# Order and places of the V-half moves in a fused attention and token-mixing kernel

## The chip, the cores and the metric

The kernel runs on one core of one Trainium2 chip. A core has a matrix engine (TensorE, "PE" in the profile; its weight loads are shown apart as "PEld"), a vector engine (VectorE, "DVE"), a scalar engine for activations (ScalarE, "ACT"), a general engine (GpSimd, "POOL"), and a sync engine (SyncE, "SP") that in this kernel does nothing but issue DMA transfers. Each engine works through its own instruction queue in order and waits on semaphores for the others.

The metric is the device time of one execution in microseconds, taken as the median over several runs.

## The reference

The input x has 2048 tokens of width 512, in bfloat16. Two branches are computed from it and mixed by a gate for each token:

```python
g = sigmoid((x * gate_w).sum(-1, keepdims=True))
a = attention(x)      # 32 heads of width 16, sliding window of 256 tokens, causal
b = token_mlp(x)      # layernorm, then a two-layer MLP over the token axis, hidden size 1376, gelu
return g * a + (1 - g) * b
```

The attention projects x to q, k and v with one 512 x 1536 matrix. A query at token i sees the keys at i-255 to i. Its softmax output is multiplied by wo (512 x 512). The token MLP multiplies by w1 (2048 x 1376) and w2 (1376 x 2048) along the token axis.

## The kernel before

**Tiles.** Tokens are cut into 16 tiles of 128. The attention's queries are handled in blocks j that are shifted by half a tile, so that block j has the queries of the tokens 128 j + 64 to 128 j + 191. Such a block needs the keys of tile j whole ("A") and of tile j-1 whole ("B"), with a triangle masked away in part of each, and two corners ("C"): the first 64 keys of tile j+1 ("D"), and the last 64 keys of tile j-2 ("F"). For each block the score products `s` run on PE, the exponentials `e` on ACT, the masks `m` on DVE or POOL, then the products with V, named `pvj.0` to `pvj.3` (line 1158, with the matmuls at line 1087), and then the steps `n1` to `n4` on DVE, which transpose, normalise and put the output into the tile `xo`. `n1` (line 1178) is what reads the PV products' accumulator.

**V's halves.** V lies in the tile `VA`, one slot for each token tile, 17 columns for each head (16 of V and a column of ones, which gives the softmax's denominator). For a block with both corners (j = 2 to 14), the two corners are multiplied together: the weights for one head are a column of 128 rows whose upper 64 rows come from the first half of V's tile j+1 and whose lower 64 rows come from the second half of tile j-2. There are two forms of it, each with the other half of the rows blank, and they lie in a tile `VZ` with three places (`NVZ = 3`, line 354). The blanks are written once (lines 580 and 581). For each block one task `vzj` (lines 725 to 732) issues two DMA transfers from `VA` to `VZ`, of 64 partitions each:

```python
nc.sync.dma_start(buf(b)[0:HB, 0, :], VA[0:HB, t_, :]),            # line 727, t_ = j + 1
nc.sync.dma_start(buf(b)[HB:P, 1, :], VA[HB:P, t_ - 3, :]),        # line 728, tile j - 2
```

The task waits for the copies `vc` that bring V's tiles j+1 and j-2 from PSUM into `VA` (line 709), for the blanks, and for its place: a place is free again when the PV products of the block that had it before are done. The readers of a place are the steps `pvj.1` and `pvj.3`, those of the "B" halves (lines 1149 to 1156); their matmuls and weight loads are the ones on `VZ` at line 1087.

**Order.** The order of the work on each engine is written out by hand, as five strings of task names in `PLAN` (lines 189 to 277). A digit after a colon is the place of a ring that the task takes: `vz6:0` is the move for block 6, into place 0 of `VZ`. The function `arrange` (line 85) walks the five queues with a table of estimated costs. It never changes the order within a queue; it only merges the five queues into one order of emission, in which dependences are then worked out. The estimated times have one more use (lines 1325 to 1330): where a POOL task's start is estimated within 1 us of the end of a DVE task that uses both of DVE's ports, a wait of POOL on that task is added.

**The SP queue.** It starts with loads of x, the weights and w1 (names `w1_gi`: column group g, token quarter i), between which the half swaps `vs` and the first `vz` moves stand. Then come the loads of w2 (`w2_0` to `w2_2`), which go into the space of w1 and so wait until the first MLP layer's products `u` on that group are done, the load of wo, and the stores of the outputs (`o0` to `o15r`), each of which waits for its last step `f` on DVE or ACT. Between these the remaining `vz` moves stand. As every queue, SP's is in order: a `vz` task whose place isn't free yet holds up all that stands behind it.

Before the change the 13 moves take the places like this: place 2 belongs to `vz12` alone, which is issued third; place 1 to `vz2`, `vz3`, `vz8` and `vz14`; place 0 to the other eight (4, 5, 6, 7, 9, 10, 11, 13).

On PE the second half of the schedule mixes the attention of later blocks with the MLP's second layer (`y` chains, line 669, also the line of the projections and of the first layer). The PV products run in the order of the blocks.

Of the kernel before, what the change touches and what calls it, by code (L numbers as in the profile page):

```python
# [84 lines left out]
def arrange(tasks):  # L85
# [21 lines left out]
    while len(order) < len(tasks):  # L107
# [163 lines left out]
    """,  # L271
    SP="""
        x0.0 x0.2 wqk0 wqk1 wqk2 wqk3 x1.4 xt1 wv x2.8 bias xt3 x3.12 xt2 vs0 w1_02 w1_03 vs1 w1_22 vs2 gw w1_12
        w1_23 w1_01 w1_00 w1_10 w1_11 vz2:1 w1_13 vz12:2 vz4:0 vz3:1 w1_20 w1_21 vz8:1 vz5:0 vz6:0 w2_0 vz7:0 w2_1
        w2_2 vz9:0 wo o0 o4 vz14:1 o8 o7 vz10:0 vs13 o2 o9 o1 vz11:0 o5 o10 vz13:0 o11 o3 o6 o12 o14 o13 o15l o15r
    """,
)

# [1096 lines left out]
```

## Time and profile before

| what | value |
|---|---|
| time, median of 4 runs | 200.53 us (199.89 to 201.4) |
| the profiled execution | 199.89 us, span 198.2 us from the first instruction to the last |
| granted TensorE clock | 1.000 |
| busy in the span: PE, ACT, DVE, POOL | 188.7, 169.4, 156.5, 79.8 us |
| moves to `VZ` | 26 DMA issues of 70.0 KB, 2.5 us in the median from issue to landing |
| loads of weights from `VZ` on PE | 832, 13.2 us busy |

The table's busy times are those of the page's first part. An engine's idle time is listed with the instruction before which it lay and with what released it; the queue of SP is listed by itself ("SPq"), as starts and durations of the DMA issues, and its waits are not part of any engine's idle time. A time "to landing" runs from the start of the issue to the transfer's end. In the timeline, starts are in us from the start of the span; a matmul's line is "output <- moving operand, weights".

### The profile page before, as it was taken

What the parts mean: (1) busy time and instruction counts of PE and PEld (TensorE: products, weight loads), DVE (VectorE), ACT (ScalarE), POOL (GpSimd) and SP (SyncE); (2) the same over time, 40 slices, a digit from 0 to 9 for tenths busy, and PEclk for the clock granted to TensorE, in tenths of its full rate; (3) what the DMA queues carried; (4) which work ended last, traced back from release to release, by engine and by line L of the source; (5) the groups of instructions that cost most, each with busy time, mean ns of one, the idle gap of its engine ahead of it and who ended that gap; (6) DMA issues with size and microseconds to landing.
All of it is one profiled execution on the core that took longest, in us unless ns stands there. A gap on an engine that the chain in (4) does not pass through costs nothing. (4 is left out here: it accounts for less than half of the span.)

```text
span 198.2 us, 9066 instructions
## 1 busy us (share of the span) xinstructions
PE 188.7 (95%) x4026; PEld 93.2 (47%) x4058; DVE 156.5 (79%) x318; ACT 169.4 (85%) x198; POOL 79.8 (40%) x118
## 2 busy tenths in 40 slices
PE   7999999999999999999999999999999999999993
PEld 3644444443535445445534554344445354554572
DVE  1898988879988978985689789636767868869683
ACT  2379999999897997998899899899899989899632
POOL 6395897326325351113323200055069335551310
PEclk9999999999999999999999999999999999999999
DMA  5999899940061001001499760010212020100002
GB/s 166 297 291 217 180 279 332 329 135 5 3 174 32 3 0 32 3 5 32 126 345 385 275 185 7 26 55 30 67 38 71 18 71 19 33 30 29 31 7 79
DMA packets 23189, 22.02 MB, mean 111 GB/s; under 512 B 7566, under 2 KB 21262, under 8 KB 23150
## 3 DMA queue, kind: packets, MB, share of 16 engines
q1 hardware_dynamic: 23150, 21.44, 37.0%
q8 instruction: 32, 0.52, 1.1%
q14 instruction: 7, 0.06, 0.1%
HBM read 15.61 MB, written 2.10 MB: 89 GB/s over the span
## 5 line engine op out<-in xcount | busy, mean ns | idle before, releaser
L893 ACT ACTIVATE et<-ps 128x1024 bf16<-128x1024 f32 (+1 forms) x94 | 89.6, 1017 | 6.0 <-PE ps L941 2.2
L535 POOL TENSOR_SCALAR_AFFINE_SELECT et<-et 128x512 bf16<-128x512 bf16 (+2 forms) x63 | 46.6, 750 | 55.4 <-ACT et L893 34.6
L893 ACT ACTIVATE XT<-ps 128x1024 bf16<-128x1024 f32 (+1 forms) x60 | 58.3, 1013 | 7.8 <-PE ps L941 4.7
L669 PEld LDWEIGHTS <-wb 128*32 128x32 bf16 (+4 forms) x645 | 31.9, 97 | 34.5 <-issue 6.5
L669 PE MATMUL pb<-ug,wb 128*32 128x512 bf16 (+5 forms) x377 | 43.8, 366 | 1.1 <-issue 1.0
L669 PE MATMUL pb<-h,wb 128*128 128x512 bf16 (+2 forms) x251 | 42.6, 381 | 1.3 <-issue 1.3
L535 POOL TENSOR_SCALAR_AFFINE_SELECT XT<-XT 128x512 bf16<-128x512 bf16 (+1 forms) x28 | 20.0, 719 | 47.1 <-ACT XT L893 28.1
L669 PE MATMUL pb<-XT,wqkv 128*128 128x512 bf16 (+2 forms) x184 | 31.1, 370 | 1.3 <-ACT XT L893 0.4
L1178 DVE STREAM_TRANSPOSE et<-ps 128x1024 f32<-128x1024 f32 (+1 forms) x17 | 20.1, 1183 | 12.3 <-PE ps L1087 11.6
L1087 PEld LDWEIGHTS <-VA 128*32 128x32 bf16 (+1 forms) x1056 | 20.1, 97 | 6.5 <-issue 1.3
L941 PE MATMUL ps<-QZ,KT 32*128 32x256 bf16 (+1 forms) x496 | 23.1, 265 | 0.0
L753 DVE TENSOR_TENSOR QZ<-pb,par 128x1024 bf16<-128x1024 f32 x16 | 19.5, 1221 | 2.4 <-PE pb L669 2.3
L669 PEld LDWEIGHTS <-wqkv 128*128 128x128 bf16 (+1 forms) x190 | 12.6, 97 | 14.5 <-DMA wqkv<-in_A_wqkv_dram 0.5
L1087 PE MATMUL ps<-et,VA 128*32 128x128 bf16 (+2 forms) x624 | 18.0, 218 | 0.0
L669 PE MATMUL pb<-wo,xo 128*32 128x512 bf16 (+2 forms) x148 | 17.2, 375 | 0.2
L941 PEld LDWEIGHTS <-KT 32*128 32x128 bf16 x496 | 7.4, 92 | 20.6 <-ACT et L893 10.6
L669 PE MATMUL pb<-wqkv,XT 128*128 128x512 bf16 (+1 forms) x65 | 15.4, 380 | 0.8 <-issue 0.5
L973 DVE TENSOR_TENSOR et<-et,mask 128x512 bf16<-128x512 bf16 x26 | 13.3, 510 | 2.5 <-ACT et L893 2.4
L440 DVE TENSOR_SCALAR ot<-pb,c,c 128x512 bf16<-128x512 f32 (+1 forms) x11 | 8.6, 784 | 7.4 <-PE pb L669 7.4
L1087 PE MATMUL ps<-XT,VA 128*32 128x128 bf16 (+2 forms) x432 | 13.9, 215 | 0.0
L1087 PEld LDWEIGHTS <-VZ 128*32 128x32 bf16 x832 | 13.2, 98 | 0.9 <-DMA VZ<-VA 0.3
L769 DVE BATCH_NORM_STATS2 stats<-xo 128x6 f32<-128x512 bf16 x16 | 10.8, 683 | 3.3 <-DMA xo<-in_A_x_dram 3.3
(76 smaller groups left out, 199.4 us busy)
## 6 DMA issues: line engine op xcount, KB each, us to landing
wb<-in_B_w_dram SPq DMA_DIRECT2D x8, 512.0 KB, 8.3
wb<-in_B_w_dram SPq DMA_DIRECT2D x2, 2048.0 KB
VZ<-VA SPq DMA_DIRECT2D x26, 70.0 KB, 2.5
xo<-in_A_x_dram SPq DMA_DIRECT2D x3, 512.0 KB, 5.4
out_dram<-ot SPq DMA_DIRECT2D x12, 128.0 KB, 2.1
wb<-in_B_w_dram SPq DMA_DIRECT2D x4, 352.0 KB, 5.8
wqkv<-in_A_wqkv_dram SPq DMA_DIRECT2D x4, 256.0 KB, 4.6
wb<-in_B_w_dram SPq DMA_DIRECT2D x1, 1024.0 KB, 5.4
```

The source lines that it names most:

```text
L440: return nc.vector.tensor_scalar(out=out_, in0=in_, scalar1=scale, scalar2=bias, op0=ALU.mult, op1=ALU.add)
L535: return nc.gpsimd.affine_select(out=out_, in_=in_, pattern=[[0, n] for n in pattern] + [[step, HB]], compare_op=op, fill=0.0, base=base_, ...
L669: made.append(nc.tensor.matmul(buf(b)[c:z_, c0:c0 + w_], lhsT=lhsT[:, c:z_], rhs=rhs, start=(j == 0), stop=(j == n - 1), skip_group_check= ...
L753: lambda k=k, b=b: nc.vector.tensor_tensor(out=QZ[:, k, :, (i % NQ) * SB:(i % NQ + 1) * SB], in0=buf(b)[:, None, :].to_broadcast([P, 2, SB ...
L769: f"bs{t_}", {"DVE": 0.67}, lambda b=b, t_=t_: nc.vector.bn_stats(buf(b)[:], xo[:, t_, :]),
L893: lambda e=e, b=b, shape=shape: nc.scalar.activation(out=shape(buf(e)), in_=shape(buf(b)), func=ACT.Exp, scale=SCALE),
L941: made.append(nc.tensor.matmul(to[:, :, done:done + m], lhsT=keys(j if x == "A" else j - 1, k)[rows], rhs=q[rows], start=True, stop=True, ...
L973: made.append(nc.vector.tensor_tensor(out=v, in0=v, in1=m.to_broadcast(list(v.shape)), op=ALU.mult))
L1087: return lambda: nc.tensor.matmul(to(), lhsT=v() if callable(v) else v, rhs=buf(e)[rows, col:col + n], start=first, stop=last, tile_positi ...
L1178: lambda: nc.vector.transpose(out=view(buf(tr).bitcast(FP32)), in_=view(buf(o))), [last], takes=[tr], uses=[o],
```

## The change

Only the SP string of `PLAN` changes. The same 26 DMA transfers are issued with the same sizes, and the other four strings are as before.

```diff
     SP="""
         x0.0 x0.2 wqk0 wqk1 wqk2 wqk3 x1.4 xt1 wv x2.8 bias xt3 x3.12 xt2 vs0 w1_02 w1_03 vs1 w1_22 vs2 gw w1_12
-        w1_23 w1_01 w1_00 w1_10 w1_11 vz2:1 w1_13 vz12:2 vz4:0 vz3:1 w1_20 w1_21 vz8:1 vz5:0 vz6:0 w2_0 vz7:0 w2_1
-        w2_2 vz9:0 wo o0 o4 vz14:1 o8 o7 vz10:0 vs13 o2 o9 o1 vz11:0 o5 o10 vz13:0 o11 o3 o6 o12 o14 o13 o15l o15r
+        w1_23 w1_01 w1_00 w1_10 w1_11 vz2:0 w1_13 vz3:1 vz4:2 vz5:0 w1_20 w1_21 vz6:1 vz8:0 w2_0 vz7:2 w2_1 w2_2
+        vz9:1 wo o0 o4 o8 o7 vz10:2 vs13 o2 o9 o1 vz11:0 vz12:1 o5 o10 vz13:2 o11 vz14:0 o3 o6 o12 o14 o13 o15l
+        o15r
     """,
```

The moves now take the places in the order 0, 1, 2 by the number of their block: 2, 5, 8, 11, 14 have place 0; 3, 6, 9, 12 place 1; 4, 7, 10, 13 place 2. They are issued in the order of the blocks, but for `vz8`, which stands before `w2_0` and `vz7`. Each move now waits for the PV products of the block three before it. `vz3`, `vz5` and `vz6` stand earlier in the queue than they did, `vz8`, `vz12` and `vz14` later.

## Prediction

> **What bounds the kernel now.** I read the busy times first, then the granted clock, then who waited for what is written to `VZ`, and last the timeline around the place found. The page's first two parts:
>
> ```profile
> PE 188.7 (95%) x4026; PEld 93.2 (47%) x4058; DVE 156.5 (79%) x318; ACT 169.4 (85%) x198; POOL 79.8 (40%) x118
> ...
> PE   7999999999999999999999999999999999999993
> ...
> ACT  2379999999897997998899899899899989899632
> ...
> PEclk9999999999999999999999999999999999999999
> DMA  5999899940061001001499760010212020100002
> ```
>
> PE is busy in every slice but the first and the last. With 198.2 us of span it has 9.5 us of idle time in all, 1.8 of them before 10 us (busy 8.18 of 10.00) and 3.3 after 186 us (busy 8.87 of 12.20). ACT is second and close. The DMA engines are busy up to about 45 us and again from 95 to 119 us, and nearly idle elsewhere. So an edit to the DMA queue can show only in a wait that PE, or ACT ahead of PE, has on it. The list of waits over all engines, and the page's group of weight loads from `VZ`, say how much of that there is:
>
> ```profile
> L1087 PEld LDWEIGHTS <-VZ 128*32 128x32 bf16 x832 | 13.2, 98 | 0.9 <-DMA VZ<-VA 0.3
> ```
>
> ```profile
> PEld L1087 <- DMA VZ<-VA: 0.3, 1, 0.3
> ```
>
> Of 26 moves one was waited for, once, for 0.3 us. That is the whole of what the moves cost PE in this execution. The timeline shows where:
>
> ```profile
> 89.92 0.40 PE L941 MATMUL ps<-QZ,KT 32*128 32x256 bf16 x8
> 90.01 0.46 SPq L727 DMA_DIRECT2D VZ<-VA  x1
> ...
> 90.57 1.10 SPq L728 DMA_DIRECT2D VZ<-VA  x1
> ...
> 92.77 0.11 PEld L1087 LDWEIGHTS <-VZ 128*32 128x32 bf16 x4
> 92.83 0.54 PE L1087 MATMUL ps<-et,VZ 128*32 128x64 bf16 x8
> 93.15 0.10 PEld L1087 LDWEIGHTS <-VZ 128*32 128x32 bf16 x4 [0.27 <-DMA VZ<-VA]
> ```
>
> This is `vz6`. It has to wait for place 0 until pv5 is done (89.9 us), is issued at 90.01 and 90.57, and pv6 wants it at 92.8. The first half (line 727) is there; the second lands about 2.5 us after its issue, and PE stands still for 0.27 us. The rest of SP's moves show how the queue stands to PE:
>
> ```profile
> 36.00 0.82 SPq L727 DMA_DIRECT2D VZ<-VA  x1
> ...
> 53.38 0.46 SPq L727 DMA_DIRECT2D VZ<-VA  x1
> ...
> 62.13 0.47 SPq L727 DMA_DIRECT2D VZ<-VA  x1
> ...
> 75.78 0.46 SPq L727 DMA_DIRECT2D VZ<-VA  x1
> ...
> 129.92 0.47 SPq L727 DMA_DIRECT2D VZ<-VA  x1
> ```
>
> By the order of the string these are `vz12`, `vz3` (after pv2), `vz8` (after pv3), `vz5` (after pv4) and `vz14`.
>
> **The change part by part.** Each move is placed by what released it before, and held against the first weight load that reads it.
>
> Early part. `vz2` stays at 33.6. `vz3` goes where `vz12` was, at 36.0; it needs V's tile 4, whose copy on ACT (33.35 us, 0.61 long) is done by then. `vz4` stays at 37.6. `vz5` takes the turn of `vz3`: both wait for pv2, so it goes at 53.4, and `w1_20` and `w1_21`, which stand right behind in both versions, stay at 54.7. Wanted: pv3 at 60.7, pv4 at 74.5, pv5 at 88.7. The slowest landing of any move was 8.9 us, the early ones took 4.5 to 7.8, so all are there with over 12 us to spare.
>
> Middle part. `vz6` takes the turn of `vz8` (after pv3, 62.1): landed by about 65, 28 us before pv6 wants it. `vz8` takes the turn of `vz6`, after pv5 at 90.0, and is wanted at 117.2. `w2_0` (95.76), `vz7` (96.2) and `w2_1` (102.3) wait for first-layer products that lie behind pv5 and pv6 on PE, so they do not move, nor does `vz7`'s landing (8.9 us behind `w2_0`, by 105.7; wanted at 111.5). `vz9` no longer waits for pv7 and goes right behind the last w2 load, at about 112.1 for 112.8, and the load of wo with it (wanted at 124.7).
>
> Late part. `vz10` (139.6) and `vz11` (151.4) follow `o7` and `o1`, and keep their times within some tenths. `vz12` comes behind `vz11`, at about 153; its place was given back after pv9 (139.5), it lands by 163 even at 8.9 us, and is wanted at 168.7. `vz13` goes at 161.4 for 161.8 (wanted 176.6). `vz14` goes behind `o11` at about 169.7, lands by 179.4 at the slowest, wanted 184.1. What stands behind them on SP: `o5`, issued at 160.03, has 6 us of cover for the two issues of `vz12` (0.5 each, 1.9 at the longest row); `o3`, issued at 172.86, has 3 us for those of `vz14`. The stores' only followers are the output buffers, and the last store is set by PE's end.
>
> So the sum: issues of SP are 26 as before, each hidden behind SP's own waiting; no wait on POOL, DVE or ACT is touched, since their strings are as before. (The waits that `arrange` adds for POOL go by its estimates. They would shift if a move's estimated end set a start on PE; the table gives a move 0.6 us and 2.0 us to land, and the trace has 2.8 us from pv5's end to the first load of pv6 from `VZ`, so the tightest move doesn't set one. I count nothing for it.) Removed: 0.27 us on PE at 93 us, once. After it the next link is ACT, which at 95.3 us had waited 0.57 us for PE, so it moves along; from 98.9 to 110.5 ACT has no gap of its own and PE's score products follow it, so the 0.27 us passes on. I take it whole: 199.89 - 0.27 = 199.6 for an execution like the profiled one. That one was the fastest of four, 0.64 us under their median; taken from the median the sum is 200.53 - 0.27 = 200.26, said as 200.3.
>
> What the profile does not show is the same wait in the other executions. From below it is nothing (0.27 us less of landing time would do). From above: if all of the 0.64 us by which the median lies above the profiled run were waiting at pv6, the gain would be 0.91, and 199.62 the time; if the landing went to the 4.4 us that `vz9` took, the wait would be 0.27 + 1.9 = 2.2. Landings away from loads spread over 1.9 to 3.4 us, so I take the profiled 0.27 and keep 0.91 for the range.
>
> A second thing not shown is a semaphore wait of PE that the old order had made needless: with `vz12` and `vz14` issued long before, their arrival may have been implied by waits for later transfers, and the new order would give PE up to four waits more (two halves each). Satisfied waits on `VZ` leave no gap in the trace (eight loads in 0.16 us throughout), so the lower end is nothing; the upper end is the 0.42 us that a switch between forms shows on PEld, four times, 1.7 us. The nearest rows are the gapless ones, since they are of the same instructions; I take nothing.
>
> [...]
>
> **The rivals.**
>
> *Nothing is gained (200.5).* The 0.27 us is taken up by the next wait. For it: between 110 and 117 us PE waits for ACT's last scores (0.41 us before 113.5), and ACT's chain up to the gelu has hardly a gap. Against it: ACT itself waited for PE at 95.3, so its chain starts earlier too.
>
> *Faster by over 0.5% (199.5 or less).* `vz6` was the only move with less than 5 us between landing and use, and the profiled execution is the fastest one. If the others owe their extra time to a later landing there, 0.91 us and a little more goes: 199.2 to 199.6. Against it: 0.64 us of scatter is what any kernel of this length could show, and nothing in the trace ties it to this move.
>
> *Slower by over 0.5% (201.5 or more).* The added PE waits at pv12 and pv14. At 0.42 us for each of four, less 0.27, the time is 200.53 + 1.68 - 0.27 = 201.9; it decides for "slower" only from 0.32 us each, (1.0 + 0.27) / 4. For it: PE has so little idle time that any new gap is paid in full. Against it: the gapless loads of the other eleven blocks, which wait for their moves too.
>
> **How the numbers follow.** 0.5% is 1.0 us, about what a measurement of this kernel can tell from no change. The forecast (0.27 us gained, 200.3; its own range 199.6 to 201.1 from the scatter of the runs) gets 0.53; nothing gained 0.14, which is the same verdict; faster 0.16; slower 0.17. So same has 0.67. The range from 199.2 to 201.9 goes from the low end of the faster case to the middle of the slower one, and leaves some 0.15 out.
>
> **What would show it.** Right: the weight loads from `VZ` have no wait on a DMA; `vz6` is issued near 62 us and `vz8` near 90; PE's idle time falls by about 0.3 us, between 92 and 94; the w2 loads are where they were. Wrong: a gap on PE ahead of weight loads from `VZ` at pv12 or pv14; a wait for w1 or w2 on PE because SP was held; POOL's waits on DVE other than before; stores that land late enough to hold an `f` step.

## The result and the profile after

| | before | after |
|---|---|---|
| median | 200.73 us (56 runs, 199.89 to 202.03) | 200.24 us (35 runs, 199.62 to 201.43) |
| profiled execution, span | 198.2 us | 199.0 us |

The ratio of the times is 0.9974 with a 95% interval of 0.9964 to 0.9985: the changed kernel is 0.3 to 0.7 us faster, 0.49 us by the medians. That is less than the 0.5% below which the prediction speaks of the same time.

The profiled execution of the changed kernel happens to be one of its longer ones; its span is even above that of the kernel before. So single spans can't be compared here, only the stretches in them that the change touches. The page's first parts, and its group of weight loads from `VZ`, of the changed kernel (its lines count one higher than those of before):

```profile
PE 189.5 (95%) x4026; PEld 93.7 (47%) x4058; DVE 156.4 (79%) x318; ACT 169.6 (85%) x198; POOL 79.9 (40%) x118
...
PE   7999999999999999999999999999999999999993
...
PEclk9999999999999999999999999999999999999999
...
L1088 PEld LDWEIGHTS <-VZ 128*32 128x32 bf16 x832 | 13.2, 98 | 0.6
```

The group's idle time is 0.6 us where it was 0.9, and no DMA is named as its releaser any more. The timeline of SP and PE at the place that mattered, in the changed kernel:

```profile
62.45 0.47 SPq L728 DMA_DIRECT2D VZ<-VA  x1
...
90.41 0.46 SPq L728 DMA_DIRECT2D VZ<-VA  x1
...
93.13 0.16 PEld L1088 LDWEIGHTS <-VZ 128*32 128x32 bf16 x8
...
154.03 0.55 SPq L728 DMA_DIRECT2D VZ<-VA  x1
```

The move at 62.45 us is now `vz6`, the one at 90.41 `vz8`, the one at 154.03 `vz12`. pv6's loads at 93.13 run on without the gap of 0.27 us that split them into four and four.

A measure that doesn't depend on how an execution began is the distance from the transpose behind pv5 to the one behind pv6, both on DVE and both released by PE's last product. Before, and then in a second profile of the changed kernel:

```profile
90.16 1.25 DVE L1178 STREAM_TRANSPOSE et<-ps 128x1024 f32<-128x1024 f32 x1 [0.91 <-PE ps L1087]
...
94.93 1.25 DVE L1178 STREAM_TRANSPOSE et<-ps 128x1024 f32<-128x1024 f32 x1 [2.16 <-PE ps L1087]
```

```profile
90.70 1.25 DVE L1179 STREAM_TRANSPOSE et<-ps 128x1024 f32<-128x1024 f32 x1 [0.90 <-PE ps L1088]
95.17 1.25 DVE L1179 STREAM_TRANSPOSE et<-ps 128x1024 f32<-128x1024 f32 x1 [1.85 <-PE ps L1088]
```

That is 4.77 us before and 4.47 us after, 0.30 us less. In the first profile of the changed kernel it is 4.62 us; there sixteen weight loads from `VA` at 93.55 us took 0.40 us, and 0.25 in the second profile, with no releaser named.

What made the first profile of the changed kernel long lies elsewhere. Its transpose behind pv5 started 0.34 us later than before, and SP's queue was late by 0.6 us at its first move already (34.20 us for 33.58). At 97.8 us PE stood still for 0.68 us more. The profile shows nothing that it waited for ("issue"):

```profile
97.83 0.10 PEld L670 LDWEIGHTS <-wb 128*32 128x32 bf16 x3 [0.68 <-issue]
```

This came in one of the three profiles of the changed kernel, so it isn't counted as part of the change. What caused it isn't shown.

### The profile page after: what moved, and what is told of

It reads as the page before. It is cut to its first block, busy times and chain, and to the rows that moved or that the text cites. A ratio compares the mean times of both kernels' runs of the same rounds, so it can differ in the third digit from the quotient of the medians.

```text
span 199.0 us, 9068 instructions
## 1 busy us (share of the span) xinstructions
PE 189.5 (95%) x4026; PEld 93.7 (47%) x4058; DVE 156.4 (79%) x318; ACT 169.6 (85%) x198; POOL 79.9 (40%) x118
```

## The experiments

The theory is that the whole gain is PE's wait at pv6. The main rival is that the rest of the change, the freer places and the late moves, gives part of it. In this section "pv5 to pv6" is the distance between the two transposes.

### Only vz6 is moved

```diff
-... vz3:1 w1_20 w1_21 vz8:1 vz5:0 vz6:0 w2_0 vz7:0 w2_1
+... vz3:1 w1_20 w1_21 vz6:1 vz5:0 w2_0 vz7:0 vz8:1 w2_1
```

The kernel before, with `vz6` in the turn and place of `vz8`, and `vz8` behind `vz7`. All other places and the early `vz12` and `vz14` stay as they were.

> The kernel before with one thing changed: vz6 takes the turn and the place of vz8 (place 1, after pv3), and vz8 goes behind vz7. Theory (the gain is the wait of PE on vz6 and nothing else): the whole gain of the change comes with this alone, ratio to before 0.996 to 0.999, as the change's 0.9974; in the profile no wait of PE on the moves. Rival (the rest of the change gives part of the gain, by other places and by what SP is held up for): the ratio stays at 0.9987, the 0.27 us of the profile of before, or nearer to 1, and the rest is in the next run.

Measured: 200.1 us, ratio 0.9981 (0.9966 to 0.9996). No wait of PE on a move; pv5 to pv6 4.50 us. One move out of its place gives as much as the whole change, within the interval; the changed kernel beside it on the same chip had 0.9978. By itself this run doesn't exclude a small part for the rest, since its interval holds the 0.9987 that 0.27 us would give.

### All but vz6

```diff
-... vz2:1 w1_13 vz12:2 vz4:0 vz3:1 w1_20 w1_21 vz8:1 vz5:0 vz6:0 w2_0 vz7:0 w2_1
-w2_2 vz9:0 wo o0 o4 vz14:1 o8 o7 vz10:0 vs13 o2 o9 o1 vz11:0 o5 o10 vz13:0 o11 o3 ...
+... vz2:1 w1_13 vz4:0 vz3:1 w1_20 w1_21 vz8:1 vz5:0 vz6:0 w2_0 vz7:0 w2_1
+w2_2 vz9:2 wo o0 o4 o8 o7 vz10:0 vs13 o2 o9 o1 vz11:1 vz12:2 o5 o10 vz13:0 o11 vz14:1 o3 ...
```

> The change without its effect on vz6: vz12 and vz14 go late, vz9 to vz14 wait for the block three before, no store or weight load stands behind a full place; but vz6 still waits for pv5 and is issued at about 90 us. Theory: as before, ratio 0.999 to 1.001, and the profile has a wait of PE on the moves at about 93 us of 0 to 0.7 us. Rival (the rest of the change gives part of the gain): 0.9975 to 0.9988.

The heading says a little too much. `vz12` (the second of the moves in the kernel before) and `vz14` go late, and `vz10` to `vz14` wait for the block three before; the place of `vz9` is free from the start. But `vz3`, `vz5`, `vz7` and `vz8` keep the turns they had. Their part is covered by the kernel above, which has `vz3` and `vz5` where they were and still has the gain.

Measured: 200.61 us, ratio 1.0013 (0.9994 to 1.0033). The gap at pv6 is back, in the timeline of this kernel:

```profile
91.06 1.11 SPq L728 DMA_DIRECT2D VZ<-VA  x1
...
93.26 0.11 PEld L1087 LDWEIGHTS <-VZ 128*32 128x32 bf16 x4
...
93.69 0.10 PEld L1087 LDWEIGHTS <-VZ 128*32 128x32 bf16 x4 [0.32 <-DMA VZ<-VA]
```

pv5 to pv6 takes 4.82 us. With these two runs the gain is placed: it comes with `vz6` and goes with it, and the rest of the change gives nothing that these runs can measure.

### vz6 later than before

```diff
-... vz5:0 w1_20 w1_21 vz6:1 vz8:0 w2_0 vz7:2 ...
+... vz5:0 w1_20 w1_21 vz8:0 vz6:1 w2_0 vz7:2 ...
```

> The changed kernel with vz6 issued behind vz8 in place of ahead of it, so that both are issued after pv5, vz6 last. Theory: its second half is issued 1.2 to 1.7 us later than in the kernel before (91.8 to 92.3 us), lands by 94.3 to 94.8, PE waits 1.4 to 1.9 us at pv6, and the time is 1.4 to 1.9 us over the changed kernel's, ratio to before 1.0045 to 1.007. Rival (a wait at pv6 is taken up further on, where PE waits for ACT): under 0.7 us over the changed kernel's, ratio below 1.001, although the profile shows the wait.

Measured: 202.14 us, ratio 1.0083 (1.0051 to 1.0116), above the 1.0045 to 1.007 expected. The timeline of its profiled execution:

```profile
92.69 0.60 SPq L728 DMA_DIRECT2D VZ<-VA  x1
...
93.33 0.60 SPq L729 DMA_DIRECT2D VZ<-VA  x1
...
94.77 0.10 PEld L1088 LDWEIGHTS <-VZ 128*32 128x32 bf16 x4 [1.17 <-DMA VZ<-VA]
...
95.45 0.10 PEld L1088 LDWEIGHTS <-VZ 128*32 128x32 bf16 x4 [0.58 <-DMA VZ<-VA]
```

PE waits 1.17 + 0.58 = 1.75 us, inside the 1.4 to 1.9 expected, though partly by luck: the second half was issued at 93.33 us, 1.0 us behind the latest time expected, while PE came to pv6 some 0.8 us later than before and the half landed faster (PE started 2.1 us behind its issue, 2.6 in the first profile of before). The four executions with a granted clock of 0.999 or 1.000 took 201.14 to 202.18 us, 201.8 in the mean, 1.6 us over the 200.2 of the changed kernel beside them and 1.006 of the kernel before; so a wait at pv6 is passed on to the end, nearly whole, and not taken up by ACT. The other two took 203.59 and 204.46 us at a mean granted clock of 0.991 and 0.989, which lifts the ratio. The profiled one is the first of these, and its windows (columns: length and PE busy, PEld, DVE, ACT and POOL busy, each with its number of instructions, then the granted clock and the DMA engines' share and GB/s) show what was added:

```profile
94.00:95.00 1.00, 0.21 (x4) 0.10 (x4) 0.00 (x0) 1.00 (x2) 0.27 (x1) 1.00 0.53 135
95.00:96.00 1.00, 0.55 (x44) 0.55 (x48) 0.00 (x0) 0.48 (x1) 0.00 (x0) 0.86 0.01 1
96.00:97.00 1.00, 1.00 (x36) 0.68 (x28) 0.00 (x0) 0.00 (x0) 0.00 (x0) 0.50 0.07 16
97.00:98.00 1.00, 1.00 (x48) 0.81 (x44) 0.00 (x0) 0.00 (x0) 0.00 (x0) 0.50 0.00 0
98.00:99.00 1.00, 1.00 (x37) 0.61 (x29) 0.66 (x1) 0.05 (x1) 0.00 (x0) 0.50 0.00 0
99.00:100.00 1.00, 1.00 (x20) 0.41 (x16) 1.00 (x2) 1.00 (x2) 0.00 (x0) 0.93 0.00 0
```

Right behind the wait the granted clock goes to 0.50 for some 3.4 us, by the clock's means of 0.86 at 95 us, three windows of 0.50 and 0.93 at 99 us. PE's work takes twice its time there (the groups of four products on `VA` start 0.22 us apart from 97.19 us on, 0.11 at 95.49). Over 3.4 us that is a loss of 1.7 us, an estimate, and this execution took 1.8 us more than the mean of the four. This was not in the expectation.

### vz6 later still

```diff
-... w1_20 w1_21 vz6:1 vz8:0 w2_0 vz7:2 ... vz10:2 vs13 o2 ...
+... w1_20 w1_21 vz8:0 vs13 vz6:1 w2_0 vz7:2 ... vz10:2 o2 ...
```

> The changed kernel with vz6 issued behind vz8 and behind the two swaps of vs13, so about 1.2 us later still than in the run before (its second half at about 94.5 us). Theory (a wait of PE costs its own length): PE waits 2.8 to 3.2 us at pv6, the time is that much over the changed kernel's, ratio to before 1.011 to 1.014. Rival, from the run before, where two executions had a granted clock of 0.99 and were 1.8 to 2.7 us longer than the rest (a long wait of PE is followed by a stretch at a lower clock): the granted clock falls to 0.5 behind the wait for 2 to 4 us in most executions, and the time is 4 to 6 us over the changed kernel's, ratio 1.018 to 1.028.

Measured: 203.62 us, ratio 1.015 (1.0118 to 1.0183). The profiled execution waits 2.42 + 0.54 = 2.96 us at pv6, and its granted clock stays at 1.00 behind the wait (every window up to 186 us shows 1.00, so its mean of 0.997 comes from behind that):

```profile
95.61 0.10 PEld L1088 LDWEIGHTS <-VZ 128*32 128x32 bf16 x4 [2.42 <-DMA VZ<-VA]
...
96.25 0.10 PEld L1088 LDWEIGHTS <-VZ 128*32 128x32 bf16 x4 [0.54 <-DMA VZ<-VA]
```

Two of the four executions took 203.11 and 203.16 us, 2.9 us over the 200.24 of the changed kernel (which was not run beside them), about the wait alone; two took 204.87 and 204.09 us at a mean clock of 0.992 and 0.991. So the rival, that the clock falls in most executions, is not borne out, and neither is a clean "costs its own length", whose 1.011 to 1.014 was passed as well. Six of the ten executions of these two kernels show about the wait alone; four were 1.0 to 2.7 us longer, at a lower mean clock. Only one of the four was profiled, the one shown above, so for the other three a fall of the clock behind the wait is a guess from their mean clocks of 0.989 to 0.992 and not shown.

### The moves left out

```diff
-                if has_d(j) and has_f(j):
+                if j > 5 and has_d(j) and has_f(j):
+                    zb[j], sready["z", j] = zb[j - 3], sready["z", j - 3]
+                elif has_d(j) and has_f(j):
                     zb[j] = vzr.use()
```

The strings of SP lose `vz6` to `vz14`.

> The changed kernel with the moves for blocks 6 to 14 left out: those blocks multiply with the halves of block j-3 in the same place, so their corners are computed with the wrong V. All other work is as in the changed kernel, and 18 transfers with their waits on SP are gone. Theory (beyond pv6 the moves cost nothing): as the changed kernel, ratio to before 0.996 to 0.999. Rival (the moves still cost something, by SP's queue, by the transfers beside the compute, or by PE's waits that are met): 0.3 us or more under the changed kernel, ratio below 0.996.

Measured: 200.62 us, ratio 0.9992 (0.9978 to 1.0007), just outside the 0.996 to 0.999 expected, so nothing is gained over the changed kernel; if anything some is lost, which neither theory had. It was run again, beside the changed kernel on one chip:

> The kernel with the moves for blocks 6 to 14 left out (their corners computed with the wrong V), once more, since it came out at 0.9992 where 0.996 to 0.999 was expected. Theory (beyond pv6 the moves cost nothing, and the last result was scatter): ratio to before within 0.001 of that of the changed kernel beside it. Rival (without the moves something else waits, by 0.3 us): again 0.9985 to 1.0005, and 0.001 to 0.002 over the changed kernel beside it.

Measured: 200.41 us, ratio 0.9974 (0.9946 to 1.0003).

> The changed kernel once more, on the same chip as the run above. Theory and rival alike: 0.9964 to 0.9985; in the profile, from the start of the transpose behind pv5 to that behind pv6 4.45 to 4.65 us, as in the two profiles of it so far, where the order before has 4.75 to 5.2.

Measured: 200.47 us, ratio 0.9964 (0.994 to 0.9988), pv5 to pv6 4.47 us. The ratios are 0.001 apart, the edge between theory and rival, but the medians, 200.41 and 200.47 us, are nearly equal: one execution of the first kernel took 202.6 us, at a mean clock of 0.992. So the first 0.9992 was probably scatter; the intervals don't exclude the rival's 0.3 us. That anything is gained by leaving out the 18 transfers, their waits and their part of SP's queue isn't seen in either run.

### The changed kernel and the kernel before, once more

> The changed kernel itself, beside the others on the same chip. Theory and rival alike: ratio 0.9964 to 0.9985. In the profile: whether the 0.7 us that PE waited for its own instructions at 97.8 us, just behind the issue of the first load of w2, comes again at that place (then it belongs to the new order) or not.

Measured: 200.18 us, ratio 0.9978 (0.9961 to 0.9995). The 0.68 us at 97.8 us are not there.

> The kernel before itself (with one line break more in its plan), for a second profile. If the gain over 0.27 us is real and comes from pv6, PE's wait there is longer than 0.27 us in this execution, up to 0.7 us. If it is 0.2 to 0.35 us again, the wait is worth about 0.3 us in every execution.

> The same once more, for a third profile, with the same readings.

One execution each, 200.58 and 202.1 us. The waits at pv6, first of the one and then of the other:

```profile
93.61 0.10 PEld L1088 LDWEIGHTS <-VZ 128*32 128x32 bf16 x4 [0.24 <-DMA VZ<-VA]
```

```profile
91.75 1.50 SPq L729 DMA_DIRECT2D VZ<-VA  x1
...
94.73 0.10 PEld L1088 LDWEIGHTS <-VZ 128*32 128x32 bf16 x4 [0.66 <-DMA VZ<-VA]
```

So the wait is not the same in every execution. In the long one SP took 1.50 us over the issue of the second half (1.10 in the first profile of before, 1.07 in the shorter of these two), and PE's start came 2.98 us behind that issue (91.75 to 94.73) where it was 2.58 in the first (90.57 to 93.15). All profiles, by whether `vz6` was issued late or early:

| order | wait at pv6, us | pv5 to pv6, us |
|---|---|---|
| before, first profile | 0.27 | 4.77 |
| before, second | 0.24 | 4.75 |
| before, third | 0.66 | 5.19 |
| all but vz6 | 0.32 | 4.82 |
| mean of these four | 0.37 | 4.88 |
| after, three profiles | 0 | 4.62, 4.47, 4.47 |
| only vz6 | 0 | 4.50 |
| moves left out, two profiles | 0 | 4.50, 4.50 |
| mean of these six | 0 | 4.51 |

By the waits and by the distances alike, the late `vz6` costs 0.37 us in the mean of these few profiles. Without the third of before it is 0.28 by the waits and 0.27 by the distances.

## Why the prediction was right

**The place.** Shown. The forecast put the gain at one wait of PE, at pv6, and at nothing else. Moving `vz6` alone gives 0.9981, the late moves without `vz6` give 1.0013, and no move was waited for in any profile with `vz6` early. One of its signs is not there as written: PE's idle time in all was 9.5 us in the first profile of before and is 9.5 in that of the changed kernel, because of the 0.68 us at 97.8. The 0.30 us show in the stretch from pv5 to pv6.

**The size.** This term came out too small: 0.27 us said, 0.49 measured by the medians, with an interval of 0.3 to 0.7. 0.27 us was taken from one profile, that of the fastest of the four executions then shown. In three of the four profiles of the late order the wait is 0.24 to 0.32 us, about as said; the mean of 0.37 rests on the fourth, 0.66 us in an execution of 202.1 us. Nor does the wait simply grow with the time: it was 0.24 in an execution of 200.58 us. How often a wait like 0.66 comes isn't shown, and so it stays open whether such waits or scatter fill the gap from 0.27 to 0.49. The upper bound of 0.91 held. The prediction had said that the wait in the other executions wasn't shown, and took the low row all the same.

**The time.** That 200.26 was forecast and 200.24 measured is luck. The median of four runs from which the sum started, 200.53, lay 0.20 us under that of the 56, 200.73, and the gain was 0.22 us larger than said; the two nearly cancel.

**That it passes on.** Shown. ACT's idle time ahead of its exponentials at 95.3 us was 0.57 us before and is 0.27 in the second profile of the changed kernel (0.41 in the first): ACT had been waiting for PE and starts earlier by as much.

```profile
95.29 3.78 ACT L893 ACTIVATE XT<-ps 128x1024 bf16<-128x1024 f32 x4 [0.57 <-PE ps L941]
```

```profile
95.53 3.77 ACT L894 ACTIVATE XT<-ps 128x1024 bf16<-128x1024 f32 x4 [0.27 <-PE ps L942]
```

The two kernels with a longer wait lose nearly the whole of it at the end, 1.6 of 1.75 us and 2.9 of 2.96. So the rival "nothing is gained" falls.

**Added waits on PE.** The programs differ in this as the rival for "slower" feared: PE's instruction stream has 26 waits for transfers into `VZ` where it had 22. Two of the four new ones are at pv12 and one at pv14, as feared, and one at pv8. The profiles of the changed kernel have no gap on a move at any block. A wait that has been met when PE comes to it cost nothing visible here (eight loads in 0.16 to 0.17 us), as the gapless loads had suggested; the 0.42 us that the prediction set as the upper end for each didn't come.

**The queue.** The moves went where the prediction put them: 62.5 us for `vz6`, 90.4 for `vz8`, 154 for `vz12`, 170.5 for `vz14`, and `o3`, with 173.65, was not held up by it. The load of wo followed the last load of w2 after 1.6 us where it had been 2.3. POOL's stream is the same instruction for instruction, its added waits too.

**The landing.** From the issue of the second half to PE's start it was 2.6 us in the first profile of before (90.57 to 93.15) and 3.0 in the third (91.75 to 94.73). The 2.5 us that the trace gave for the landing fit the first and were short for the third.

**Faster by over 0.5%.** It did not come. Its mechanism, that slower executions wait longer at pv6, is seen in one profile, 0.66 us in the execution of 202.1 us, and not in that of 200.58 us. That execution was longer for other reasons too: its transpose behind pv5 started at 91.33 us against 90.16, ahead of pv6. So of the 2.2 us by which it is longer than the first one, 1.2 lie ahead of pv6 and 0.4 are the wait.

**Two readings.** Without effect on the sum, the prediction misread two rows. `vz6` was not the only move with less than 5 us between landing and use: the second half of `vz3`, issued at 53.94 us, landed after 2.3 us and was read from 60.74, 4.5 us later. And the DMA engines were not nearly idle between 45 and 95 us throughout; from 55 to 60 us their share was 0.57.

## What to carry to other kernels

Look for the transfer with the least time between its landing and its use; here one of 26 landed after its use was due, and only moving that one gave a gain that could be measured. A wait that one profile shows at the edge (a landing within a few tenths of the use) differs between executions (0.24 to 0.66 us in the four profiles here): take a second and a third profile before pricing it. And a forecast of a time starts from a median of few runs, whose scatter can hide an error in the gain. Places of a ring that are held long by early issues make the others queue; here that cost something at one move only, `vz6`, whose place was given back at 89.9 us and whose use came at 92.8.

## What was not expected

After PE had waited 1.75 us in two parts, the granted clock fell to 0.50 for some 3.4 us in the one execution of that kernel that was profiled; one more of its six had a mean clock of 0.989. After 2.96 us it stayed at 1.00 in the one profile there is, and two of that kernel's four executions had a mean clock of 0.99. One execution of the kernel with the moves left out had 0.992 as well, without a wait at pv6 in that kernel's profiles, so a low mean clock alone doesn't show where the fall was.

What decides whether the clock falls isn't shown. In the 3.42 us before the fall (92.30 to 95.72, worked out from the windows) PE was busy for 1.95 us. In the kernel with the wait of 2.96 us it was busy for only 0.75 us of an equally long stretch around its wait (93.00 to 96.42), and no fall followed. No profile shows a fall of the clock behind a wait of 0.66 us or less at pv6.
